# Filler matmuls ahead of the last V block, and a reordered tail, in a decode kernel of attention and a gated feed-forward

## The chip, the core and the metric

The kernel runs on one core of a Trainium2 chip. The metric is device time in microseconds: the median of several runs. One more execution, taken with the hardware profiler, gives the trace; all durations below are from that one.

## The reference

One token, x of 512 numbers, goes through two branches, and a gate mixes them. 32 query heads share 8 key/value heads (groups), four to a group; the caches have 32768 positions of 128 numbers, in bf16.

```python
q = (x @ wq)                                   # 32 heads of 128
p = softmax(q . k_cache / sqrt(128))           # per head, over 32768 positions
a = (p @ v_cache).reshape(4096) @ wo           # wo: 4096 x 512
b = (silu(x @ w_gate) * (x @ w_up)) @ w_down   # w_down: 1792 x 512
g = sigmoid((x * gate_w).sum())
out = g * a + (1 - g) * b                      # 512 numbers
```

## The kernel before

All loads are issued by SyncE (SP) on one queue, in program order: wq, x, gate_w, w_gate, w_up, and then the caches in blocks of 16384 positions (4 MB each, two blocks of K and two of V to a group). SP waits for the page a block goes into to be free. The last entries of that queue are: V block 0 of the last group, wo's first piece (rows 0 to 8 of 32 row groups of 128), V block 1, all of w_down, and wo's other four pieces (cuts 8, 18, 26, 31, 32). A row group of wo is 128 x 512.

TensorE (PE) runs a loop over groups in which it does K of group g and V of group g - 1 block by block. K blocks: PE transposes the page (L392), VectorE (DVE) copies each transpose out of PSUM (L671), PE multiplies by the queries (L404). ScalarE (ACT) takes the exponentials (L548). V blocks: 32 matmuls (L448), each 16 columns of weights against 512 columns of V, on four strips of the array in turn (output partitions 0, 32, 64, 96), accumulate in `ps_o`. ACT copies `ps_o` into `acc` (L560), and `emit_reduce` (L430) sums its rows and strips by four fp32 matmuls, which the trace lists as eight.

In the loop's last turn there are only the two V blocks and then `emit_end` (L481):

1. The softmax sums (L483) and the last reduce (L430). DVE copies the result (L665), scales it (L700) and transposes it (L707).
2. Meanwhile on PE, w_down: 14 wide matmuls (L460), one column of weights against 512 columns, on four strips in turn, into the bank `ps_w`, which DVE cleared earlier (L691).
3. A small matmul (L498) that permutes the attention output, and DVE's copy of it to `O2` (L709).
4. wo. Its row groups 0 to 17 are wide matmuls too (L460), added to `ps_w`. DVE copies `ps_w` to `part` (L711).
5. The other 14 row groups are "rows" (L471): four matmuls of 128 columns each, one to each quarter of the output, on the four strips of `ps_c`. So the result is four rows of 128 numbers, at partitions 0, 32, 64, 96. After the third piece's rows, four fp32 matmuls (listed as eight) with the constant `sel4` add the strips of `part` to the four rows. The fourth and the last piece follow.
6. DVE copies `ps_c` to `res_row` (L713), SP and ACT store two rows each (L206), one DMA to a row, and GpSimd (POOL) waits for all four.

Each piece of wo has its own semaphore, on which PE waits ahead of that piece's matmuls. PE's order is the program's order: what stands behind a waiting instruction waits too.

## Time and profile before

| what | us |
|---|---|
| median of 3 runs (lowest to highest) | 353.35 (353.26 to 353.37) |
| profiled execution | 354.17 |
| its span, first to last instruction | 352.4 |
| PE busy, DVE busy, ACT busy | 269.4, 178.5, 32.3 |
| mean granted PE clock | 0.845 |
| DMA over the span | 148.23 MB, 421 GB/s |
| last V page landed | 337.06 |
| last V block on PE | 337.18 to 340.80 |
| result copied (L713) | 349.99 to 350.28 |

All positions are microseconds from the start of the span. The profile's page gives each engine's busy time, the queues, and the chain of work that ended last; the trace can also be asked for the chain in order of time, for the instructions of a stretch, and for the busy time of each engine and PE's granted clock in stretches of one's choice (1.00 is the full clock). "x32" counts instructions. PE busy counts a matmul up to its modelled end, and matmuls overlap, so neighbouring lines of PE can overlap a little. A wait is put down to what came last. DMA "to landing" is from the issue to the semaphore.

### The profile page before, as it was taken

The page shows a single profiled execution, that of the slowest core. Times are in us where ns is not written, and L with a number is a line of the kernel's source. Part 1 is how long each engine was busy: PE and PEld are TensorE (multiplying, and loading weights), DVE is VectorE, ACT ScalarE, POOL GpSimd, SP SyncE. Part 2 cuts the span into 40 slices and gives each one's busy share as a digit, 9 for nine tenths or more (in the row PEclk, how much of TensorE's full clock was granted, in tenths as well). Part 3 has the DMA queues.
Part 4 walks back from the last instruction along what each step waited for, and adds up shares of the span by engine and source line. Part 5 has one row for each costly group of instructions (what it writes and reads, how often), then busy time and mean ns, then how long its engine had stood idle before and what let it go on. Part 6 is the DMA issues. An engine that isn't in the chain of part 4 may idle for free.

```text
span 352.4 us, 8926 instructions
## 1 busy us (share of the span) xinstructions
PE 269.4 (76%) x4005; PEld 231.1 (66%) x4005; DVE 178.5 (51%) x204; ACT 32.3 (9%) x148; POOL 5.8 (2%) x24
## 2 busy tenths in 40 slices
PE   0446986997999959697798959795997859695376
PEld 0446976976687949395786849494966759593033
DVE  0310967655683938266562828274655728193001
ACT  1000000400120040002100040003000030004000
POOL 0200000000000000000000000000000000000000
PEclk9999988789898998769885978679887969898656
DMA  8999999999999999999999999999999999999994
GB/s 331 411 432 426 445 433 416 430 424 450 420 432 424 450 421 428 424 450 420 432 424 450 420 432 424 450 420 432 424 450 420 432 424 450 420 432 420 439 402 163
DMA packets 5924, 148.23 MB, mean 421 GB/s; under 512 B 666, under 2 KB 796, under 8 KB 924
## 3 DMA queue, kind: packets, MB, share of 16 engines
q1 hardware_dynamic: 5912, 148.12, 98.2%
q8 instruction: 6, 0.10, 0.1%
q14 instruction: 2, 0.02, 0.0%
q10 hardware_dynamic: 4, 0.00, 0.0%
HBM read 148.11 MB, written 0.00 MB: 420 GB/s over the span
## 4 chain that ended last, share of the span: by engine, by line
DMA 58%; PE 36%; DVE 3%; issue 1%; SPq 1%; ACT 0%; ACTq 0%
DMA page<-in_A_k_cache_dram 54%; PE pst L392 25%; PE ps_sc L404 6%; DMA page<-in_A_v_cache_dram 5%; PE ps_o L448 3%; DVE ktT L671 3%; PE pst L460 1%; PE ps_m L430 1%; PE pst L471 1%; SPq L302 0%; ACT acc L560 0%; SPq L298 0%; SPq L299 0%; DVE res_row L713 0%; SPq L300 0%
## 5 line engine op out<-in xcount | busy, mean ns | idle before, releaser
L671 DVE COPY ktT<-pst 128x2048 bf16<-128x2048 bf16 x128 | 155.8, 1224 | 106.6 <-PE pst L392 99.6
L392 PE MATMUL pst<-ident_f,page 128*128 128x128 f32 x1024 | 158.2, 311 | 41.5 <-DMA page<-in_A_k_cache_dram 39.2
L392 PEld LDWEIGHTS pst<-ident_f,page 128*128 128x128 f32 x1024 | 134.6, 161 | 53.0 <-DMA page<-in_A_k_cache_dram 47.0
L404 PEld LDWEIGHTS ps_sc<-qcur,ktT 128*128 128x128 bf16 x2048 | 67.1, 97 | 11.4 <-DVE ktT L671 10.0
L404 PE MATMUL ps_sc<-qcur,ktT 128*128 128x8 bf16 x2048 | 67.9, 166 | 8.6 <-DVE ktT L671 8.6
L448 PE MATMUL ps_o<-page,ET 128*16 128x512 bf16 x512 | 43.0, 495 | 7.9 <-DMA page<-in_A_v_cache_dram 7.9
L448 PEld LDWEIGHTS ps_o<-page,ET 128*16 128x16 bf16 x512 | 13.5, 105 | 26.7 <-issue 20.3
L539 ACT ACTIVATE nbias<-gmax 128x4 f32<-128x4 f32 x8 | 1.6, 205 | 263.2 <-POOL gmax L273 263.2
L548 ACT ACTIVATE ET<-ps_sc,nbias 128x128 bf16<-128x128 f32 x64 | 24.1, 553 | 0.7
L548 ACT ACTIVATION_READ_ACCUMULATOR ET<-ps_sc,nbias 128x1 f32 x64 | 18.1, 282 | 0.0
L676 DVE TENSOR_REDUCE pmaxf<-ps_sc 128x4 f32<-128x512 f32 x16 | 11.1, 692 | 11.5 <-PE ps_sc L404 11.5
L430 PE MATMUL ps_m<-sel,acc 128*128 128x4 f32 x72 | 11.4, 282 | 3.7 <-ACT acc L560 3.7
L430 PEld LDWEIGHTS ps_m<-sel,acc 128*128 128x128 f32 x72 | 10.8, 229 | 4.3 <-ACT acc L560 4.3
L340 PE MATMUL ps_m<-ones_bf,x_row 1*128 1x1 bf16 x4 | 0.3, 172 | 13.6 <-DMA gw_row<-in_gate_w_dram 13.6
L377 PE MATMUL ps_m<-xT,page 128*128 128x1 bf16 x112 | 6.9, 198 | 4.2 <-DMA page<-in_B_w_up_dram 4.2
L377 PEld LDWEIGHTS ps_m<-xT,page 128*128 128x128 bf16 x112 | 6.8, 159 | 4.3 <-DMA page<-in_B_w_up_dram 4.3
L340 PEld LDWEIGHTS ps_m<-ones_bf,x_row 1*128 1x128 bf16 x4 | 0.2, 114 | 13.6 <-DMA gw_row<-in_gate_w_dram 13.6
L694 DVE RECIPROCAL rS<-pst 128x32 f32<-128x32 f32 x1 | 0.4, 358 | 15.3 <-PE pst L483 15.3
L273 POOL PARTITION_ALL_REDUCE gmax<-pmax x8 | 3.0, 372 | 291.7 <-DVE pmax L678 291.7
L560 ACT ACTIVATE acc<-ps_o 128x512 f32<-128x512 f32 x8 | 5.2, 650 | 17.0 <-PE ps_o L448 17.0
L585 DVE CAST xT<-ps_m 128x4 bf16<-128x4 f32 x1 | 0.2, 163 | 12.5 <-PE ps_m L340 12.5
L353 PE MATMUL ps_m<-xT,page 128*128 128x1 bf16 x128 | 3.6, 165 | 0.3 <-DVE gwT L586 0.3
(68 smaller groups left out, 33.6 us busy)
## 6 DMA issues: line engine op xcount, KB each, us to landing
page<-in_A_k_cache_dram SPq DMA_DIRECT2D x16, 4096.0 KB, 26.9
page<-in_A_v_cache_dram SPq DMA_DIRECT2D x16, 4096.0 KB, 31.2
page<-in_A_wq_dram SPq DMA_DIRECT2D x1, 4096.0 KB, 12.4
page<-in_A_wo_dram SPq DMA_DIRECT2D x2, 1024.0 KB, 24.7
page<-in_B_w_gate_dram SPq DMA_DIRECT2D x1, 1792.0 KB, 15.7
page<-in_B_w_up_dram SPq DMA_DIRECT2D x1, 1792.0 KB, 20.5
wd<-in_B_w_down_dram SPq DMA_DIRECT2D x1, 1792.0 KB, 20.5
page<-in_A_wo_dram SPq DMA_DIRECT2D x1, 1280.0 KB, 23.1
```

What stands on the lines that cost most here:

```text
L353: ins = pe.matmul(ps_m[:, M_Q0 + h : M_Q0 + h + 1], wq_v[:, c, h * DH : (h + 1) * DH], xT[:, c : c + 1], start=(c == 0), stop=(c == KC - 1),)
L377: ins = pe.matmul(ps_m[:, base + j : base + j + 1], wgu[:, w, c, :].rearrange("d (p j) -> d j p", j=FC)[:, j, :], xT[:, c : c + 1], start= ...
L392: ins = pe.transpose(pst[u % NST][:, k * 128 : (k + 1) * 128], kv[:, n * 128 : (n + 1) * 128], ident_f[:, :],)
L404: ins = pe.matmul(ps_sc[b][:, col : col + 2 * HPG], kt[:, k, e, :], qcur[:, e, :], start=(e == 0), stop=(e == 1),)
L430: ins = pe.matmul(ps_m[:, M_P0 : M_P0 + HPG], acc[:, q, :], sel4[:, q * HPG : (q + 1) * HPG], start=(q == 0), stop=(q == RQ - 1),)
L448: ins = pe.matmul(ps_o[32 * c : 32 * c + RQ * HPG, :], ET[:, n : n + RQ, :].rearrange("p n h -> p (n h)"), view[:, k * RQ : (k + 1) * RQ, ...
L460: return pe.matmul(ps_w[32 * c : 32 * c + 1, :], vec[:, j : j + 1], w[:, j, :], start=first, stop=last, skip_group_check=True,)
L471: ins = pe.matmul(ps_c[32 * oc : 32 * oc + 1, 0:128], lhs, rhs[:, oc * 128 : (oc + 1) * 128], start=first, stop=last, skip_group_check=True,)
L548: act.activation(ET[:, b * R : (b + 1) * R, h], sc[:, h, :], ACT.Exp, bias=nbias[:, g, h : h + 1], scale=SCALE, accum_out=esum[:, g, b, h ...
L560: act.activation(acc[:, :, :].rearrange("p q d -> p (q d)"), ps_o[:, :], ACT.Copy).then_inc(sem_acc, STEP)
L671: dve.tensor_copy(ktT[:, u % NKT, :], pst[u % NST][:, :].bitcast(BF16)).then_inc(sem_cp, 1)
L676: dve.tensor_reduce(pmaxf[:, b, :], sc, AX.X, ALU.max).then_inc(sem_pmax, 4)
```

## The change

- `emit_warm`: ahead of the last V block only, PE runs 18 matmuls (a loop of 9 turns of two) of the 128 x 128 identity against 512 columns of an old transpose buffer, into a half of a PSUM buffer that nobody reads. They wait for nothing.
- w_down's 14 wide matmuls move behind wo's first piece; the first of wo's matmuls now starts the accumulation.
- The rows use two strips with two output rows each, instead of four with one. For that the weights have two columns, the vector in one and zero in the other (`O2z`, filled by two more DVE copies; `sel5` with a zero column for the strips of `part`). Each row group is still four matmuls of 128 columns.
- The part matmuls now start the accumulation of the rows, directly behind wo's second piece; before, they stood behind the third.
- wo's last cut is at 30 instead of 31.
- SP and ACT store once each, two rows to a DMA. DVE copies 34 partitions of the result instead of 128.
- At the start: one cleared column and one cleared small tile more on DVE.

```diff
-    WO_CUTS = [0, 8, 18, 26, 31, 32]
-    WIDE = WO_CUTS[2]
+    WO_CUTS = [0, 8, 18, 26, 30, 32]
+    KW = 1
+    WIDE = WO_CUTS[KW + 1]
+    NWARM = 18
+    RPS = 2
...
+        ps_d = pst[1][:, 512:1024]
...
         def store(eng, k):
-            for c in (2 * k, 2 * k + 1):
-                eng.dma_start(
-                    out[0, :, 128 * c : 128 * (c + 1)], res_row[32 * c : 32 * c + 1, :]
-                ).then_inc(sem_out, 16)
+            n = RPS * 128
+            eng.dma_start(
+                out[0, 0, n * k : n * (k + 1)].rearrange("(c n) -> c n", c=RPS),
+                res_row[32 * k : 32 * k + RPS, :],
+            ).then_inc(sem_out, 16)
...
                 def emit_rows(lhs, rhs, first, last):
-                    for oc in range(OC):
-                        ins = pe.matmul(
-                            ps_c[32 * oc : 32 * oc + 1, 0:128],
-                            lhs,
-                            rhs[:, oc * 128 : (oc + 1) * 128],
-                            start=first,
-                            stop=last,
-                            skip_group_check=True,
-                        )
+                    for e in range(RPS):
+                        for k in range(OC // RPS):
+                            oc = RPS * k + e
+                            ins = pe.matmul(
+                                ps_c[32 * k : 32 * k + RPS, 0:128],
+                                lhs(e),
+                                rhs[:, oc * 128 : (oc + 1) * 128],
+                                start=first and e == 0,
+                                stop=last and e == RPS - 1,
+                                skip_group_check=True,
+                            )
                     return ins
+
+                def emit_warm():
+                    with pe.Fori(0, NWARM, 2):
+                        for _ in range(2):
+                            pe.matmul(ps_d, ident[:, :], ktT[:, 0, 0:512], start=True, stop=True)
...
-                    pe.wait_ge(sem_dve_tT, 1)
-                    pe.wait_ge(sem_ld_wd, 16)
-                    pe.wait_ge(sem_psw, 1)
-                    for j in range(FC):
-                        emit_wide(wd, tT, j, j < NSTRIP, False)
...
                     for k, s in enumerate(sem_wo):
+                        if k == 0:
+                            pe.wait_ge(sem_psw, 1)
+                        if k == 1:
+                            pe.wait_ge(sem_dve_tT, 1)
+                            pe.wait_ge(sem_ld_wd, 16)
+                            for j in range(FC):
+                                emit_wide(wd, tT, j, False, False)
                         pe.wait_ge(s, 16)
...
-                        if k == 1:
+                        if k == KW:
                             ins.then_inc(sem_pe_w, 1)
-                        if k == 2:
                             pe.wait_ge(sem_dve_w, 1)
-                            emit_rows(sel4[:, 0:1], part[:, :], False, False)
+                            pe.wait_ge(sem_dve_oz, RPS)
+                            emit_rows(lambda e: sel5[:, 1 - e : 3 - e], part, True, False)
...
+                        if b == NB - 1:
+                            with pe.If(i > (G - 1) * STEP):
+                                emit_warm()
                         with pe.If(i > 0):
                             emit_v(i, b)
...
                 dve.tensor_copy(O2[:, :], ps_m[:, M_O0 : M_O0 + WOJ]).then_inc(sem_dve_O2, 1)
+                for e in range(RPS):
+                    dve.tensor_copy(
+                        O2z[:, :, e, e], ps_m[:, M_O0 + WIDE : M_O0 + WOJ]
+                    ).then_inc(sem_dve_oz, 1)
                 dve.wait_ge(sem_pe_w, 1)
                 dve.tensor_copy(part[:, :], ps_w[:, :]).then_inc(sem_dve_w, 1)
                 dve.wait_ge(sem_pe_sum, 1)
-                dve.tensor_copy(res_row[:, :], ps_c[:, 0:128]).then_inc(sem_dve_row, 1)
+                dve.tensor_copy(res_row[0 : 32 + RPS, :], ps_c[0 : 32 + RPS, 0:128]).then_inc(sem_dve_row, 1)
```

More of the change, by code (lines that the diff above doesn't have):

```diff
@@ L58, in bass_gated_mix__gqa_block_cached__swiglu_ffn__decode_kernel @@
     assert KC * H * DH <= PAGE and 2 * KC * F <= PAGE and WOJ * NOUT <= PAGE
-    WO_CUTS = [0, 8, 18, 26, 31, 32]
-    WIDE = WO_CUTS[2]
+    WO_CUTS = [0, 8, 18, 26, 30, 32]
+    KW = 1
+    WIDE = WO_CUTS[KW + 1]
+    NWARM = 18
     OC = NOUT // 128
     RQ = 4
-    N_SEL = 12
+    N_SEL = 13
     NSTRIP = 4
+    RPS = 2
     assert RQ * HPG <= 32 and RQ * DH == 512
@@ L112, in bass_gated_mix__gqa_block_cached__swiglu_ffn__decode_kernel @@
         sem_dve_O2 = S_("s_dve_O2")
+        sem_dve_oz = S_("s_dve_oz")
         sem_dve_row = S_("s_dve_row")
@@ L166, in bass_gated_mix__gqa_block_cached__swiglu_ffn__decode_kernel @@
         esum2 = T("esum2", [128, G, HPG], FP32)
-        sel4 = T("sel4", [128, 16], FP32)
+        sel5 = T("sel5", [128, 17], FP32)
+        sel4 = sel5[:, 1:17]
         acc = T("acc", [128, RQ, DH], FP32)
@@ L174, in bass_gated_mix__gqa_block_cached__swiglu_ffn__decode_kernel @@
         O2 = T("O2", [128, WOJ], BF16)
+        O2z = T("O2z", [128, WOJ - WIDE, RPS, RPS], BF16)
         part = T("part", [128, NOUT], FP32)
@@ L275, in _ @@
                     ).then_inc(sem_gmax, 1)
-                pool.wait_ge(sem_out, 64)
+                pool.wait_ge(sem_out, 32)
             @block.sync
@@ L505, in emit_end @@
                             if j < WIDE:
-                                ins = emit_wide(wo_v, O2, j, False, j >= WIDE - NSTRIP)
+                                ins = emit_wide(wo_v, O2, j, j < NSTRIP, j >= WIDE - NSTRIP)
                             else:
                                 ins = emit_rows(
-                                    O2[:, j : j + 1], wo_v[:, j, :], j == WIDE, j == WOJ - 1
+                                    lambda e: O2z[:, j - WIDE, e, :],
+                                    wo_v[:, j, :],
+                                    False,
+                                    j == WOJ - 1,
                                 )
-                        if k == 1:
+                        if k == KW:
                             ins.then_inc(sem_pe_w, 1)
-                        if k == 2:
                             pe.wait_ge(sem_dve_w, 1)
-                            emit_rows(sel4[:, 0:1], part[:, :], False, False)
+                            pe.wait_ge(sem_dve_oz, RPS)
+                            emit_rows(lambda e: sel5[:, 1 - e : 3 - e], part, True, False)
                     ins.then_inc(sem_pe_sum, 1)
@@ L615, in _ @@
                 dve.wait_ge(sem_ident, 1)
-                dchain(dve.tensor_copy(sel4[:, :], ident[:, 0:16]))
+                dve.memset(O2z[:, :, :, :], 0.0)
+                dchain(dve.memset(sel5[:, 0:1], 0.0))
+                dchain(dve.tensor_copy(sel4, ident[:, 0:16]))
                 for c in range(1, NSTRIP):
@@ L619, in _ @@
                         dve.tensor_tensor(
-                            sel4[:, :], sel4[:, :], ident[:, 32 * c : 32 * c + 16], ALU.add
+                            sel4, sel4, ident[:, 32 * c : 32 * c + 16], ALU.add
                         )
```

## The prediction

> **What bounds the kernel now.** I read the page first: its queue table, then the chain by line. The first line is the load queue, with its share of the DMA engines' time over the span; the others are the chain, by engine.

> ```profile
> q1 hardware_dynamic: 5912, 148.12, 98.2%
> ...
> DMA 58%; PE 36%; DVE 3%; issue 1%; SPq 1%; ACT 0%; ACTq 0%
> ```

> The queue is busy for nearly the whole span, and the change removes no byte of load. PE's 36% lies in stretches that the next load hides, except the last one. So I went to the chain in order of time, from the last V page on (start, us, what).

> ```profile
> 318.58 1.86 PE ps_o L448 x32
> ...
> 320.46 16.60 DMA page<-in_A_v_cache_dram
> 337.06 0.12 issue
> 337.18 3.62 PE ps_o L448 x32
> ...
> 340.87 0.61 ACT acc L560
> ...
> 341.52 1.87 PE ps_m L430 x8
> 343.39 1.80 PE pst L460 x11
> ...
> 345.61 1.98 PE pst L460 x17
> 347.59 2.37 PE pst L471 x53
> ...
> 349.99 0.29 DVE res_row L713
> ```

> From 337.06, when the last V page lands, to 349.99 PE and what it feeds set the end, and only this stretch can pay. The same 32 matmuls take 1.86 us at 318.58 and 3.62 us at 337.18. The reduce (L430) takes 1.87 us here, while the timeline has it at 1.03 us at 75.51. Everything in the tail runs at half rate.

> The DMA issues give landings, as start plus time to landing: w_down 320.83 + 20.5 = 341.3, wo's second piece 321.31 + 23.1 = 344.4, third 347.0, fourth 348.6, last 322.7 + 26.1 = 348.8. The last piece's few matmuls could end near 349.2, and PE ends near 349.95. At most 0.75 us can be won on PE, whatever its clock.

> ```profile
> 319.08:322.50 3.42, 1.34 (x28) 0.40 (x16) 0.75 (x4) 2.24 (x13) 0.37 (x1) 1.00 0.87 374
> 322.50:325.91 3.41, 1.98 (x12) 1.89 (x16) 0.68 (x3) 1.37 (x7) 0.00 (x0) 0.50 1.03 435
> 325.91:329.32 3.41, 3.41 (x32) 0.87 (x24) 0.15 (x1) 0.00 (x0) 0.00 (x0) 0.50 1.07 459
> 329.32:332.74 3.42, 0.00 (x0) 0.00 (x0) 0.00 (x0) 0.00 (x0) 0.00 (x0) 1.00 1.00 431
> 332.74:336.15 3.41, 0.00 (x0) 0.00 (x0) 0.00 (x0) 0.00 (x0) 0.00 (x0) 0.50 0.90 384
> 336.15:339.56 3.41, 2.38 (x24) 0.88 (x28) 0.00 (x0) 0.00 (x0) 0.00 (x0) 0.50 0.98 417
> ```

> A window's clock follows from the window before it. 1.34 us of work loses the full clock, 3.41 wins it, 0.00 loses it, 2.38 does not win it. Elsewhere 13 transposes at half clock with 2.76 us win it (46.02) and 13 with 2.68 do not (226.92); at full clock 1.33 us of transposes loses it (264.47) and 1.74 keeps it (80.15). So about 0.8 of a window wins, and less than 0.4 to 0.5 loses; I count with 0.45. The window edges are the same 3.41 us apart everywhere but nothing in the trace ties them to the kernel's start, so I take their place as free from one execution to the next.

> **The change, part by part.** I first take PE at half clock, as traced, then the 18 matmuls.

> *w_down behind wo's first piece.* Before, its 14 matmuls (343.32 on, 14 x 0.107 = 1.50 us of streaming, from 32 in 3.43) run beside three DVE steps, the last ending 344.16, and the small matmul L498 starts behind them at 345.12. After, L498 can start at 344.20: 0.92 earlier. Then 32 wide matmuls instead of 18 follow it, 1.50 more. Sum +0.58. The new waits are met: w_down landed at 341.3, its vector at 30.4, the cleared bank at 324.3.

> *The copy of `part` loses its cover.* Before, 32 row matmuls (347.28 to 348.76) run while DVE copies (347.95, 0.69). After, PE waits for that copy, and for two copies of O2, directly behind wo's second piece; the third piece's rows, the fourth's and the last's queue behind the wait. The part matmuls' eight passes start at 348.70 + 0.58 = 349.28, with 56 row matmuls still to run instead of 24.

> *Two strips.* Row matmuls on four strips go at 36 ns (24 in 0.86) to 46 ns (32 in 1.48). Four wide ones share 427 ns, so one strip streams 128 columns in 107 ns; on two strips that is 53 ns each, if they overlap as the wide ones do. Bounds: 36 (the strips were never the limit) and 107 (no overlap). I take 53, since V's matmuls overlap exactly so. Then 64 x 0.053 + 0.2 of latency = 3.6, end 352.9 instead of 349.96: **+2.9 us at half clock**. At 36 ns it is +1.9, at 107 ns +6.3. Cutting wo at 30 adds four matmuls (0.2) behind the last landing, already in the 56.

> *One store per queue.* The second stores start at 350.6 (SP) and 350.9 (ACT) against 350.31 for the first, and the span ends 1.3 after the last issue. Gain between 0 (a two-row store takes as long as two) and 0.6; I take 0.4.

> *DVE.* Two small copies behind O2 (0.19 each, like L709) lie beside 3.4 us of wide matmuls; without that cover 0.4. Two memsets at the start (some 0.2 each) lie before the first transposes, which wait 3.14 us for a K page. The extra branch per block lies in load waits. SP issues the same loads; the last two share the same bytes, so 348.8 stands.

> *The 18 matmuls.* 512 columns take 213 ns at full clock (half of 427). They start when V's first block has streamed, 325.73 + 3.43 = 329.16, and the clock rises at the next window edge, t later (0 to 3.41), for V's block fills the window. They end at 329.16 + 3.84 + t/2, that is 333.0 to 334.7, 2.4 to 4.1 us before the last V block. In the traced position (t = 0.16) the window to 336.15 holds 0.35 us of work, and the clock is lost 1 us before V. Going through positions of the edge with the thresholds above:

> - t under 0.45 or over 2.6 (37%): V's last block and all behind it at half clock, +2.9.
> - 0.45 to 1.15 (20%): V cold, but 2.7 us of it fill one window, the clock is back near 340.1, and the last landing binds: +0.1. (This needs no extra matmul.)
> - 1.15 to 1.85 (20%): V starts at full clock and loses it within 0.7 us, +0.7 to +1.5, take 1.1.
> - 1.85 to 2.6 (22%): V saves 0.8 to 1.4 but nothing later reaches 0.8 of a window, take +2.3.

> Weighted: 0.37 x 2.9 + 0.20 x 0.1 + 0.20 x 1.1 + 0.22 x 2.3 = 1.8. Less 0.4 for the stores: **+1.4 us**.

> [...]

> **The rivals.**

> *Slower, as above:* 18 matmuls are half of what the gap of 7.9 us takes at full clock, and PE's own order got longer.

> *Faster:* the matmuls come from a loop of two, and the trace has no short loop on PE. If a turn of it costs 0.2 us or more beyond its 0.43, nine turns reach past 335, the windows stay over 0.45 and V starts warm: 1.76 saved there, 0.84 on the reduce. Then w_down, wo's second and third pieces are met as they land, and the last landing decides. Rows after 348.8 cost 0.4 to 1.4 by the clock then granted, so PE ends between -0.7 and +0.3; with the stores -1.1 to +0.1. Against it: from scores to V at 318.0 to 318.5, PE's stream passes 32 instructions and two branches without a visible stall, and the loop can be issued while V's first block still streams (3.4 us). Two strips at 36 ns would help this case too.

> *No change within 0.2%* (0.7 us, about what a measurement of this kernel can tell from none): the edges often lie as in the second position, or the loop is slow and the tail ends on cold rows.

> *Much slower:* two strips do not overlap, 56 x 0.107 more, +3.4 on top: 357 to 359. Against it: V's four strips do.

> *The change does nothing of what it says:* the clock at V's start is 0.50 as before; that is the first position of my list.

> **The numbers.** The profiled execution took 354.17 us, span 352.4 and 1.8 around it; the median of the runs is 353.35, 0.8 less. I add the change to both: 355.6 for a profiled one, 354.7 for the median. Chances: slower as forecast 0.55, much slower 0.04, within 0.2% 0.18, faster 0.23. Slower by over 0.2% together 0.59. The forecast's own range is 354.1 to 356.0 (+0.7 to +2.6). The range over cases goes down to 352.5 (-0.85, most of the fast rival) and up to 356.0, leaving out the much slower case and the best clocks.

> **What the profile will show.** Right: 18 matmuls (L494) at some 215 ns each once the clock is up, ending before 335; the granted clock 0.50 through most of V's last block; part copy with PE idle about 1 us before it; row matmuls near 53 ns at half clock; one store per queue. Wrong: matmuls of L494 reaching past 336; V's last block in 1.9 us; row matmuls at 36 ns or less; PE waiting for wo's landings.

## The result, and the profile after

The changed kernel takes 354.43 us (median of 21 runs) against 353.54 us for the kernel before (21 runs). The ratio is 1.0030, with a 95% interval from 1.0018 to 1.0041: slower by about 0.9 to 1.1 us. Its runs are spread more widely, from 352.77 to 357.47 us, those of before from 353.26 to 354.40 (one disturbed run of before left out).

The queue and the chain on the page are as before, and the last V page lands within 0.2 us of where it did (336.88, before 337.06).

```profile
q1 hardware_dynamic: 5912, 148.12, 98.1%
...
DMA 58%; PE 37%; DVE 3%; issue 1%; SPq 1%; ACT 0%; DVEq 0%; ACTq 0%
```

The chain in order of time, from the last V page on (start, us, what):

```profile
321.05 15.83 DMA page<-in_A_v_cache_dram
336.88 0.12 issue
337.00 2.71 PE ps_o L456 x32
...
339.78 0.61 ACT acc L583
340.39 0.04 issue
340.43 1.88 PE ps_m L438 x8
...
343.62 4.02 PE pst L468 x32
347.64 0.02 issue
347.66 0.70 DVE part L740
348.37 0.04 issue
348.41 2.19 PE pst L481 x64
350.59 0.02 issue
350.62 0.28 DVE res_row L742
```

Four things are to be read here. V's last block takes 2.71 us, between the 1.9 of full clock and the 3.6 of half clock. The reduce is again at half clock (1.88). All 32 wide matmuls lie in one piece of 4.02 us behind the small matmul, and then DVE's copy of `part` stands in the chain, where it did not stand before: PE waits for it. The result's copy starts at 350.62; before, at 349.99.

Why V's block is only partly faster shows in the granted clock. This is the stage view of the changed kernel, cut at its own clock changes, every 3.41 us (columns as in the prediction: PE's busy time first, the granted clock third from the end).

```profile
327.73:331.14 3.41, 2.86 (x22) 0.98 (x17) 0.00 (x0) 0.00 (x0) 0.00 (x0) 0.50 1.03 442
331.14:334.55 3.41, 2.98 (x8) 1.31 (x14) 0.00 (x0) 0.00 (x0) 0.00 (x0) 1.00 0.89 382
334.55:337.97 3.42, 0.97 (x20) 0.53 (x24) 0.00 (x0) 0.00 (x0) 0.00 (x0) 1.00 0.97 412
337.97:341.38 3.41, 3.24 (x27) 1.79 (x16) 0.60 (x2) 0.60 (x1) 0.00 (x0) 0.50 1.01 425
...
344.79:348.21 3.42, 2.83 (x24) 0.67 (x16) 0.55 (x1) 0.00 (x0) 0.00 (x0) 0.50 0.70 277
348.21:351.62 3.41, 2.17 (x64) 1.91 (x64) 0.43 (x2) 0.00 (x0) 0.00 (x0) 1.00 0.00 0
```

The fillers end in the second window. The third holds only V's first 0.97 us, and the clock is lost at 337.97, in the middle of V's block. The last two lines show it coming back: the window from 344.79, 2.83 us busy with wide matmuls, wins it, and the row matmuls run at full clock. (The profile lists all 18 weight loads of the filler, from 329.8 to 333.9, but only 9 of its matmuls.)

### The profile page after: what moved, and what is told of

Same layout as the page of the kernel before. It is cut to its first block, busy times and chain, and to the rows that moved or that the text cites. A ratio compares the mean times of both kernels' runs of the same rounds, so it can differ in the third digit from the quotient of the medians.

```text
span 352.6 us, 8984 instructions
## 1 busy us (share of the span) xinstructions
PE 272.7 (77%) x4014; PEld 235.2 (67%) x4023; DVE 179.2 (51%) x208; ACT 32.1 (9%) x148; POOL 5.8 (2%) x24
## 3 DMA queue, kind: packets, MB, share of 16 engines
q1 hardware_dynamic: 5912, 148.12, 98.1%
## 4 chain that ended last, share of the span: by engine, by line
DMA 58%; PE 37%; DVE 3%; issue 1%; SPq 1%; ACT 0%; DVEq 0%; ACTq 0%
DMA page<-in_A_k_cache_dram 54%; PE pst L400 25%; PE ps_sc L412 6%; DMA page<-in_A_v_cache_dram 4%; PE ps_o L456 3%; DVE ktT L696 2%; PE pst L468 1%; PE ps_m L438 1%; PE pst L481 1%; SPq L310 0%; DVE part L740 0%; ACT acc L583 0%; SPq L306 0%; SPq L307 0%; DVE res_row L742 0%
## 5 line engine op out<-in xcount | busy, mean ns | idle before, releaser
L400 PE MATMUL pst<-ident_f,page 128*128 128x128 f32 x1024 | 160.2, 315 | 41.6 <-DMA page<-in_A_k_cache_dram 40.4
L400 PEld LDWEIGHTS pst<-ident_f,page 128*128 128x128 f32 x1024 | 136.6, 163 | 51.7 <-DMA page<-in_A_k_cache_dram 47.8
L456 PE MATMUL ps_o<-page,ET 128*16 128x512 bf16 x512 | 39.9, 467 | 2.6 <-DMA page<-in_A_v_cache_dram 2.5
L385 PE MATMUL ps_m<-xT,page 128*128 128x1 bf16 x112 | 6.9, 198 | 4.0 <-DMA page<-in_B_w_up_dram 4.0
L494 PE MATMUL pst<-ktT,ident 128*128 128x512 bf16 x9 | 3.7, 415 | 0.9 <-issue 0.6
```

What stands on the lines that cost most here:

```text
L385: ins = pe.matmul(ps_m[:, base + j : base + j + 1], wgu[:, w, c, :].rearrange("d (p j) -> d j p", j=FC)[:, j, :], xT[:, c : c + 1], start= ...
L400: ins = pe.transpose(pst[u % NST][:, k * 128 : (k + 1) * 128], kv[:, n * 128 : (n + 1) * 128], ident_f[:, :],)
L456: ins = pe.matmul(ps_o[32 * c : 32 * c + RQ * HPG, :], ET[:, n : n + RQ, :].rearrange("p n h -> p (n h)"), view[:, k * RQ : (k + 1) * RQ, ...
L494: pe.matmul(ps_d, ident[:, :], ktT[:, 0, 0:512], start=True, stop=True)
```

## The experiments

The theory after the result: **18 fillers are too short at full clock, so they seldom pay, and the rest of the change makes PE's own order longer.** Rivals: the fillers do pay and the rest costs far more; the fillers do harm; one of the three reorderings alone is the loss. All ratios below are against the kernel before, run on the same chip in the same job, with 95% intervals.

### No filler

```diff
-                        if b == NB - 1:
-                            with pe.If(i > (G - 1) * STEP):
-                                emit_warm()
```

> The changed kernel without its 18 filler matmuls. Theory (the filler ends some 3 us too early; the loss comes from PE's longer own order and is spread by where the clock's window edges fall): as slow as the changed kernel, 0.9 to 1.7 us over before. Rival (the filler helps V's last block in most executions and only cannot pay for the rest): clearly slower than the changed kernel, 2 us or more over before.

Measured: 354.64 us, ratio 1.0038 (1.0017 to 1.0058). That overlaps the changed kernel's 1.0030 (1.0018 to 1.0041): the 18 fillers move the time by less than these runs can show. The theory's number held, and the rival's 2 us did not come. The profiled execution (356.86 us, among the slowest three of its 12) was at half clock from 325.4 to 352.6, so it gives the price of the new order with no clock to help. The two groups of row matmuls in its timeline (start, us):

```profile
349.12 1.02 PE L481 MATMUL pst<-part,sel 128*2 128x128 f32 x8 [0.79 <-DVE part L737]
349.93 3.04 PE L481 MATMUL pst<-page,O2z 128*2 128x128 bf16 x56
```

56 on two strips in 3.04 us are 54 ns each, and the eight fp32 passes take 0.81 us up to the next start, 0.10 each. From V's start (336.81) to the result's copy (353.02) this execution needs 16.21 us; the kernel before, also at half clock, 12.81 (337.18 to 349.99). The new order costs 3.4 us when the clock stays low; of this the stores give back 0.4 behind the result's copy. The window behind which the clock could have come back is this one (stage view):

```profile
345.80:349.22 3.42, 2.63 (x22) 0.63 (x16) 0.69 (x1) 0.00 (x0) 0.00 (x0) 0.50 0.38 147
```

In the changed kernel's trace an edge lay 1.17 us behind the start of the wide matmuls (343.62, 344.79), and the window behind it was 2.83 us busy; here it lay 1.47 us behind (344.33, 345.80), and 2.63 us did not win the clock.

### 28 fillers instead of 18

```diff
-    NWARM = 18
+    NWARM = 28
```

> The changed kernel with 28 filler matmuls instead of 18, so that they reach V's last block wherever the window edges fall. Theory: V's last block always starts at full clock and takes 1.9 us; the time falls to about that of before, -0.4 to +0.4 us. Rival (the clock is not what costs, the new order is): stays 0.7 us or more over before.

Measured: 353.17 us, ratio 0.9995 (0.9982 to 1.0009), 0.35% below the changed kernel, with intervals that do not touch. The timeline shows V's last block in 1.90 us and the reduce in 1.06 us. The theory held and the rival, that the clock is not what costs, is out: too few fillers had left V's block without the full clock. V's line in the timeline:

```profile
336.62 1.90 PE L456 MATMUL ps_o<-page,ET 128*16 128x512 bf16 x32 [1.67 <-DMA page<-in_A_v_cache_dram]
```

That 28 reach V wherever the window edges fall is not shown: the three kernels here with 28 all had V in 1.90 us, but each was traced once. The stage view shows where the rest stays (from V's block on):

```profile
335.63:339.04 3.41, 2.24 (x34) 1.03 (x34) 0.14 (x1) 0.42 (x1) 0.00 (x0) 1.00 0.99 417
339.04:342.45 3.41, 2.07 (x25) 1.45 (x29) 1.39 (x8) 0.18 (x1) 0.00 (x0) 1.00 1.00 419
342.45:345.86 3.41, 2.56 (x20) 0.37 (x12) 0.43 (x1) 0.00 (x0) 0.00 (x0) 0.50 0.98 404
345.86:349.27 3.41, 3.10 (x52) 2.78 (x54) 0.26 (x1) 0.00 (x0) 0.00 (x0) 0.50 0.34 132
```

In the second window PE has the reduce, the wait for DVE's three steps and short pieces of wide matmuls. The clock is lost at 342.45, and the row matmuls, which end the kernel, run at half clock although PE had come to them 2.2 us earlier than in the changed kernel's trace (346.17 against 348.41).

### The kernel before, with fillers alone

`emit_warm` and its call, as in the change, put into the kernel before, with 28 and with 18.

> The kernel before with 28 filler matmuls ahead of the last V block, nothing else of the change. Theory: PE reaches wo earlier but then waits for its pieces, loses the clock in that wait, and ends no earlier: -0.3 to +0.3 us. Rival (PE's half clock in V's last block and the reduce is what the tail costs): -0.5 us or better.

> The kernel before with the 18 filler matmuls alone. Theory: no difference, -0.2 to +0.2 us. Rival (the 18 matmuls do harm, by their branch or by taking heat or slots): +0.5 us or more.

Measured: 28 give 353.43 us, ratio 0.9997 (0.9988 to 1.0006); 18 give 353.62 us, ratio 1.0001 (0.9991 to 1.0010). By the ratios both theories held, and harm by the 18 of the rival's size, 0.5 us or more, is out. With 28, V took 1.90 us and PE then waited, as the list of waits shows (for whom: us in total, times, longest):

```profile
PEld pst L473 <- DMA page<-in_A_wo_dram: 3.2, 2, 2.2
...
PE pst L473 <- DMA page<-in_A_wo_dram: 2.2, 2, 1.7
```

PE loses the clock in these waits (at 347.3), as expected. In this execution the tail of before is bound by wo's landings as soon as PE is faster: what the filler wins, these waits take. With 18 the profiled execution is the bad position of the window edges:

```profile
333.86:337.27 3.41, 0.44 (x2) 0.00 (x1) 0.00 (x0) 0.00 (x0) 0.00 (x0) 1.00 0.94 400
337.27:340.68 3.41, 2.52 (x25) 0.88 (x29) 0.00 (x0) 0.00 (x0) 0.00 (x0) 0.50 0.99 419
```

0.44 us of filler is left in a window, the clock goes at 337.27, and V starts at 338.16 at half clock and takes 3.59 us.

### One part of the change undone

Three kernels with 18 fillers. First, the part matmuls behind wo's third piece again:

```diff
-                                    False,
+                                    j == WIDE,
...
+                            pe.wait_ge(sem_dve_oz, RPS)
+                        if k == KW + 1:
                             pe.wait_ge(sem_dve_w, 1)
-                            pe.wait_ge(sem_dve_oz, RPS)
-                            emit_rows(lambda e: sel5[:, 1 - e : 3 - e], part, True, False)
+                            emit_rows(lambda e: sel5[:, 1 - e : 3 - e], part, False, False)
```

> The changed kernel (18 fillers), but the matmuls that add part stand behind the third piece of wo again, as before. Theory (the uncovered copy of part is the largest piece of the longer order: about 1.1 us in which PE stands still, 32 row matmuls left behind it): falls to between -0.2 and +0.5 us of before. Rival (w_down's new place or the two strips are the larger piece): stays 0.7 us or more over before.

Measured: 353.66 us, ratio 1.0021 (1.0005 to 1.0037). By the ratio (+0.2 to +1.3 us) it is slower than the theory said, by the median (+0.2) it lies inside; inconclusive.

Second, w_down ahead of the small matmul again:

```diff
+                    pe.wait_ge(sem_dve_tT, 1)
+                    pe.wait_ge(sem_ld_wd, 16)
+                    pe.wait_ge(sem_psw, 1)
+                    for j in range(FC):
+                        emit_wide(wd, tT, j, j < NSTRIP, False)
                     pe.wait_ge(sem_dve_oT2, 1)
...
```

> The changed kernel (18 fillers), but w_down's 14 matmuls stand ahead of the small matmul again, as before. Theory (its move costs 0.58 us at half clock): 0.3 to 0.6 us less than the changed kernel, that is +0.3 to +1.1 us over before. Rival (the move is the main loss): no slower than before.

Measured: 354.73 us, ratio 1.0026 (1.0008 to 1.0044). Not to be told from the changed kernel. Its profiled execution was at half clock through the tail too (335.7 to 352.7), so it can be set beside the one without fillers: from V's start to the result's copy 15.56 us (336.95 to 352.51) against 16.21. The move of w_down costs 0.65 us at half clock.

Third, four strips and four stores again (`emit_rows` and `store` of before):

> The changed kernel (18 fillers), but rows on four strips with one output row each and four stores, as before. Theory (two strips cost 0.017 us for each of 64 matmuls at half clock, 1.1 us, and the stores give 0.4 back): 0.3 to 0.7 us less than the changed kernel in the median, +0.2 to +1.1 us over before; the 56 row matmuls take 2.1 us at half clock instead of 3.0. Rival (the two strips cost nothing because LDWEIGHTS sets the pace): slower than the changed kernel by the 0.4 us of the stores.

Measured: 353.97 us, ratio 1.0013 (0.9999 to 1.0026), 0.17% less than the changed kernel, with overlapping intervals. By the ratio that is +0.5 us over before, as the theory said. Its row matmuls, at half clock (lost at 344.1):

```profile
347.41 0.61 PE L478 MATMUL pst<-part,sel 128*1 128x128 f32 x8 [0.79 <-DVE part L737]
347.79 1.72 PE L478 MATMUL pst<-page,O 128*1 128x128 bf16 x56
```

The same 56 take 1.72 us on four strips, 31 ns each (the theory had 2.1 us), against 3.04 on two. The rival, that weight loads set the pace on both, is out.

### One part of the change alone

Because the fillers' luck blurs those three, each part was also put alone into the kernel before, without fillers.

Part directly behind wo's second piece:

```diff
...
                         if k == 1:
                             ins.then_inc(sem_pe_w, 1)
-                        if k == 2:
                             pe.wait_ge(sem_dve_w, 1)
-                            emit_rows(sel4[:, 0:1], part[:, :], False, False)
+                            emit_rows(sel4[:, 0:1], part[:, :], True, False)
```

> The kernel before, but the matmuls that add part stand directly behind wo's second piece, so that nothing on PE covers DVE's copy of it. Theory (this is the largest piece of the longer order): +0.2 to +1.0 us over before. Rival (the copy's cover is worth nothing because PE waits for wo's third piece anyway): -0.2 to +0.2 us.

Measured: 353.62 us, ratio 1.0004 (0.9992 to 1.0017). The median is that of before, and the interval, -0.3 to +0.6 us, leaves only the lower part of the theory's range. Its profiled execution shows how little the lost cover can cost: PE stands still for 0.78 us, but the window with the wide matmuls wins the clock all the same (at 349.3), and 56 row matmuls take 1.16 us.

Two strips and one store per queue:

> The kernel before with rows on two strips of two output rows and one store per queue, nothing else. Theory (64 matmuls cost 1.1 us more where PE is at half clock and late, 0.4 comes back from the stores): 0.0 to +0.6 us over before. Rival (the stores pay for the strips): -0.4 to 0.0 us.

Measured: 354.56 us, ratio 1.0022 (1.0011 to 1.0033). That is +0.4 to +1.2 us: the rival, that the stores pay for the strips, is out, and the theory's upper bound of 0.6 is passed by the ratio's +0.8, which fits the dearer strips of the traces.

w_down behind wo's first piece:

> The kernel before with w_down's 14 matmuls behind wo's first piece, nothing else. Theory (0.58 us later on PE at half clock, part of it hidden behind wo's third piece): 0.0 to +0.5 us over before. Rival (the small matmul's earlier start pays): -0.4 to 0.0 us.

Measured: 354.32 us, ratio 1.0012 (0.9999 to 1.0025). By the ratio, +0.4 us, the theory's number held, but no difference at all is not quite excluded.

The three alone add up to 0.04 + 0.22 + 0.12 = 0.38%, and all three together without fillers gave 0.38%. Each interval is about 0.12% wide on either side, so the exact sum is luck. **The two strips are the largest of the three as measured, and the only one clearly over zero;** their lead over w_down's move is within the noise. The traces point the same way. With V's block at half clock in all of them, the way from V's start to the result's copy was 13.10 us with `part` early, 13.70 with two strips (whose stores give back 0.4 later) and 13.08 with w_down moved, against 12.81 before; in these three the clock came back for the last rows. At half clock throughout, the 3.4 us split into 1.7 for the strips (56 x 0.023 + 8 x 0.05), 0.65 for w_down and some 1.05 left over, in which PE's stand of 0.79 us for `part` lies. The earlier cut of wo, at 30, was not tried by itself.

### Filling the other gaps

Two versions that should keep the clock through the tail. One is the 28-filler kernel with 4 more behind the last reduce and 4 more during the copy of `part`:

```diff
...
                     emit_reduce((G + 1) * STEP)
+                    emit_fillers(4)
                     pe.wait_ge(sem_dve_oT2, 1)
...
                             ins.then_inc(sem_pe_w, 1)
+                            emit_fillers(4)
                             pe.wait_ge(sem_dve_w, 1)
```

> The changed kernel with 28 fillers, and 4 more behind the last reduce and 4 more while part is copied, unrolled, into the same unread bank. Theory (with 28 alone the clock is lost again in PE's waits at 340 to 347 and the rows run at half clock; with these gaps filled the windows stay over 0.45 and the last landing decides): -0.9 to -0.4 us of before, row matmuls at 31 ns. Rival (the fillers stand in the way of the small matmul and of the part matmuls, or the gaps for wo's pieces lose the clock anyway): -0.3 us or more.

Measured: 353.14 us, ratio 0.9987 (0.9978 to 0.9995): the only version here whose interval lies below before, by 0.13%. That is 0.2 to 0.8 us, so the theory's number is reached only in part, and against 28 fillers alone (0.9995) the step is within the noise. The stage view of its end:

```profile
335.67:339.09 3.42, 3.37 (x40) 1.34 (x38) 0.00 (x0) 0.00 (x0) 0.00 (x0) 1.00 0.98 414
339.09:342.50 3.41, 2.72 (x27) 1.67 (x23) 1.48 (x8) 0.60 (x1) 0.00 (x0) 1.00 0.99 416
342.50:345.92 3.42, 3.42 (x32) 0.98 (x32) 0.05 (x1) 0.00 (x0) 0.00 (x0) 0.50 0.98 403
345.92:349.33 3.41, 3.37 (x72) 2.15 (x68) 0.69 (x1) 0.00 (x0) 0.00 (x0) 1.00 0.38 150
```

The clock is still lost once, at 342.50, though the window before was 2.72 us busy, so it was not kept through the tail as the theory had it; but the full window of wide matmuls behind that wins it back at 345.92, in time for the rows, which take 1.98 us for 56, 35 ns each. The other version has 26 fillers, 4 behind the reduce, the part matmuls behind wo's third piece, and 6 while PE waits for that piece:

> The changed kernel with 26 fillers, the part matmuls behind wo's third piece again, 4 fillers behind the last reduce and 6 while PE waits for wo's third piece. Theory (full clock kept through the tail, part's copy covered, PE bound by wo's landings): -0.9 to -0.4 us of before, rows at 31 ns. Rival (the clock is still lost in some positions of the windows): -0.3 us or more.

Measured: 353.12 us median, ratio 0.9996 (0.9981 to 1.0010), its runs from 352.81 to 355.91. Its profiled execution lost the clock at 338.2, inside V's block. By the ratio the theory's number was missed, by the median (-0.5) it lies inside. The profile shows the rival: the clock had come up early, at 327.9, the fillers ended 3.06 us ahead of V, and the window up to 338.2 held only 1.23 us of V. Two more fillers (0.43 us) would not have closed that gap.

## Why the prediction was right, and where it was off

The sign, the cause and the range held; the size was forecast at +1.4 us and came out at +0.9 to +1.1. That it came so near is partly luck. The terms of the sum are counted from the traced execution of before (354.17 us, its tail at half clock), where the sum gives 355.6; it was added to the median of before too, which is 0.8 lower and need not have such a tail. The changed kernel's median, and its profiled execution, took 354.43: 1.2 less than the sum gives on its own base.

- *Fillers at 213 ns, ending between 333.0 and 334.7:* in the profiled execution the last one starts at 334.1 and its modelled end is 334.5. In the kernel with fillers in the gaps a full window holds 16 of their weight loads in 3.41 us: 213 ns. The fear that the loop might go slower fell: its turns follow each other without a gap (PE is busy for all 3.41 us of that window).
- *The clock by windows:* V's first block streams to 326.25 + 3.43 = 329.68 here, and the edge at 331.14 gives t = 1.46: the third position of the list, V at full clock at first and losing it within 0.7 us, end +0.7 to +1.5. It lost it after 0.97 us, and the result's copy starts 0.63 us later than before, from a V block that started 0.18 earlier: +0.8. The second position, with V cold and the clock back behind it, is seen in two variants (four strips, and `part` late), and there its price of +0.1 left something out: the clock was back near 341, but lost again at 344.1 and 344.5, after windows 2.13 and 2.31 us busy.
- *w_down, +0.58:* 0.65 at half clock.
- *Stores, 0.4:* from the end of the result's copy to the end of the span 352.4 - 350.28 = 2.1 us before, 352.6 - 350.90 = 1.7 after. Right.
- *Two strips, 53 ns:* 54. But four strips run at 31 ns, not at the 36 to 46 that I read from groups with a pause in them, and the fp32 passes cost 0.10 each on two strips, not 0.053. So the strips cost 56 x 0.023 + 8 x 0.05 = 1.7 us at half clock, not 1.1.
- *The whole new order at half clock, +2.9:* 3.4.
- **The step that was mis-sized** is the first position of the list: 37% of executions with "V's last block and all behind it at half clock, +2.9". Such an execution would end at about 356.0 or later. Two of the 21 runs do (356.18 and 357.47), not eight. The threshold was about right: at half clock, of windows without the reduce, those 2.83 us (the changed kernel) and 2.67 us (`part` late) busy won the clock, 2.62 (w_down ahead) did not, and 2.63 went both ways. The list failed in not asking it of the 32 wide matmuls, which the change puts into one piece. Counted with that estimate of 0.8 of a window, 2.73 us, a piece of 4.02 us fills one unless an edge falls 1.29 to 2.73 us behind its start; where it fills one, the rows behind it would run at full clock. The edges of the two traces above, 1.17 (won) and 1.47 us (not won) behind that start, agree. An estimate from these numbers, with the wide matmuls starting 7.52 us behind V as in the kernel without fillers: of the first position, t over 2.6 up to about 3.2 gets the clock back, and some 20% of executions, four of 21, stay at half clock. Two of so few runs is not far from that; no run here sets the position of the edges, so how often each occurs stays open.
- *The uncovered copy of `part`:* PE stands still for 0.79 us, where about 1 was forecast, but alone it cost 0.04% (-0.08 to +0.17%).
- *The rival "faster"*: its mechanism is real with 28 fillers (V in 1.90 us, reduce in 1.06) and its sum, -1.1 to +0.1, holds the measured -0.05%. Only its condition failed: the loop is not slow.
- *A sign of being wrong that did appear:* the profile shows the rows at 31 ns (56 in 1.73 us), under the 36 of the list. That is the clock, which is 1.00 from 348.21, and not the strips: at half clock they take 54.

## What to carry to other kernels

Size a filler by its time at full clock and by the whole gap it has to bridge: here 18 (3.8 us for a gap of 7.9) were worth nothing that the runs could show, 28 (6.0 us) kept the clock for V in each trace, and a clock that was kept in one place was lost again at the next waits (at 342.45 in the changed kernel with 28, at 347.3 in the kernel before with 28). Before moving work into a tail, ask which of its instructions get their speed from running side by side: going from four strips to two took the row matmuls from 31 to 54 ns at half clock and cost more (1.7 us there) than the saved stores gave (0.4). And where the clock changes at window edges that lie in another place in another trace (at 329.32 before, at 331.14 in the changed kernel, 3.41 us apart in both), compare many runs, since one profile shows only one position of them.

## What was not expected of the hardware

- What counted for the clock was not just PE's busy time in the profile. With 28 fillers, a window with 2.07 of 3.41 us busy at full clock lost it, and with the gaps filled so did one with 2.72 us; both hold the fp32 reduce (8 matmuls of 4 columns, some 1.05 us). In the changed kernel 3.24 us, with the reduce among them, did not win it. A window of transposes kept it with 1.74 us (from 80.15 in the kernel before). And at half clock two windows equally busy, 2.63 us, went different ways: with `part` early in the kernel before (345.86 to 349.27) it won the clock, without fillers (345.80 to 349.22) it did not. What is counted instead is not shown.
- Half the strips did not mean half the pace for the row matmuls: at half clock 31 ns on four strips against 54 on two, and at full clock 19 on four (32 in 0.62 us in the kernel before with 28 fillers) against 31 on two (56 in 1.73 us in the changed kernel).
- One kernel's executions were spread over 3.6 us (353.81 to 357.39, the change with no filler) where another's kept within 0.8 (353.24 to 354.08, the kernel before with 28). The places of the window edges would do this; since each was traced once, it is argued and not shown.
